# A spectral mixture and a rational expert layer: an add moved to GpSimd and two first-stage tasks moved ahead of the main loop

## Chip, cores and metric

The kernel runs on one core of a Trainium2 chip. The metric is the device time of one execution in microseconds; several executions were timed, and one was recorded by the profiler.

## What is computed

For each of 4 batches of 3008 rows and 256 columns, the reference takes a real Fourier transform over the rows, mixes the 256 columns with a complex matrix and a bias, shrinks real and imaginary part towards zero by 0.01, and transforms back. Each resulting row then goes through an expert layer with a rational activation:

```python
X = np.fft.rfft(x, axis=1)
Yr = Xr @ w_r - Xi @ w_i + b_r;  Yi = Xr @ w_i + Xi @ w_r + b_i
Yr, Yi = shrink(Yr, 0.01), shrink(Yi, 0.01)
y = np.fft.irfft(Yr + 1j * Yi, n=3008, axis=1).reshape(4 * 3008, 256)
h = y @ w_in                                   # 256 -> 2048
P = a[0] + a[1] * h + a[2] * h**2 + a[3] * h**3
Q = 1.0 + abs(b[0]) * abs(h) + abs(b[1]) * h**2
out = (P / (Q + 1e-06)) @ w_out                # 2048 -> 256
```

## The kernel before

**The transform.** 3008 = 64 x 47, and the transform of each batch is done in four stages of small matmuls. The stages of a batch pass data through DRAM twice: stage f1 writes s1, stage f2 reads it; stage i1 writes s2, the last stage (i2) reads it.

- f1 (`f1_task`, L185): 8 tasks per batch, one for each block c of 8 values of the 64. A task has 8 matmuls (L191) into two banks of PSUM, one copy by ScalarE (L155) and one by VectorE (L153) into a tile a, and stores of the tile to s1 by SyncE's DMA queue (L214 where the tile is whole, two stores; L217 where it is in parts, four stores).
- f2 (`f2_task`, L240): 12 tasks p. It reads a tile b of s1 (`load_b`, L227), does 8 matmuls (L247) and makes the tile x with ScalarE and VectorE.
- m (`m_task`, L268): 24 tasks, the mixing (L283) and shrinking.
- i1 (`i1_task`, L295): 12 tasks, stored to s2 (L308).

**The expert layer.** The result rows come in 26 groups of five blocks of 94 columns (two groups have four). For each group, `i2_task` (L338) does the last transform stage into a bank "pi" (L351), which ScalarE copies to xsh (L354) and VectorE makes into the remainder xsl (L362). For the last groups, when no transform task is left, the remainder comes from a matmul with a negative identity (L357) instead; the kernel calls such groups alone. Then 8 units per group follow, 208 in all. Unit u goes through:

- `g1_mm` (L369): 12 matmuls (L385) into h, a pair of banks; there are two such pairs. Unit 0 does its eight matmuls with xsh first, and the four with xsl after.
- `act_a` (L411), ScalarE: v = |b0 h| (L417), s = b1 h^2 (L418), then t (L421). Between them, an accumulating transfer on GpSimd's queue adds s to v (L419).
- `act_b` (L423), ScalarE: y = (v + C0)^2 (L426) and its inverse root (L428), so 1/Q.
- `dve_a` (L430), VectorE: two steps from t and h to t (L433, L434). After L434 the pair h is free for the unit after next.
- `dve_b` (L436): the high part of g (L442) and v (L444) on VectorE, t - v on GpSimd (L448), the low part of g on VectorE (L454).
- `g2_mm` (L460): 12 matmuls into the accumulators acc (L475), three iterations later.

**The order.** All engines' instructions are in an order written out by hand (`tc.manual_schedule()`). Ahead of the main loop, batch 0 goes through the whole transform, while the expert's weights are converted to high and low parts (`convert`, `from_f64`, L513 to L532; the tuples HC, HM and HF say how many steps of it come after which task). f1 tasks of batch 1 run there too: one at p = 13 (L694), and one for each entry of HF (L708 to L710). The order of blocks is 0, 1, 2, 3, 6, 7, 4, 5. Blocks 4 and 5 are loaded into the same slots as 0 and 1; these two loads wait in the list `hold` and go to SyncE's queue at the first `flush` of the loop.

The main loop (L735) has one iteration per unit, with a string that says the order of the steps: in iteration i TensorE gets the transform tasks that the planner picks (F), `g1_mm(i + 1)` and `g2_mm(i - 3)`. The planner gives each iteration a budget (`level` less the unit's own `load`) and takes tasks from the list while the spent cost stays under it; an f1 task uses both banks "ft", so there is at most one in an iteration. A task of cost 0 ends the iteration's picking. The list of batch 1 is: the f1 tasks that are left (each costs 0.95), the loads of the first two b tiles (cost 0), a pause (cost 0), f2 of p = 0 (0.86), a pause, and then f2, m and i1 tasks in turn.

**Memory.** Pools of the first part (pro, pro2, pro3; L506 to L509) are closed at L713. pro3 holds b_all (tags b0 to b3, the b tiles of batch 0), the tiles of x for batch 0, and blocks 2 and 3 of batch 1. pro holds the tiles a of the first four f1 tasks of batch 1 (the fourth in the tag "wt"). The pools mx (xsh, xsl) and mp (s, v, t, y, g) are opened on the freed space: mx lies on the beginning of pro3, mp on the rest of pro3 and on pro2 and pro. A pool's first writers wait for the closed pools that it lies on as whole pools. The pool sm stays open throughout: its tag "a" (3 slots of 128 x 512) holds parts of f1 tiles, i1 tiles and output tiles, its tag "x" (2 slots) the tiles x of later batches, f1 tiles of batches 2 and 3, and blocks 6 and 7 of batch 1.

Of the kernel before, what the change touches and what calls it, by code (L numbers as in the profile page):

```python
# [9 lines left out]
F32 = mybir.dt.float32  # L10
# [4 lines left out]
ALU = mybir.AluOpType  # L15
# [3 lines left out]
B, S, D, DFF = 4, 3008, 256, 2048  # L19
N1, N2, NG, NJ, NK = 64, 47, 2, 32, 24  # L20
ROWS = 2 * NK
JB = 5
TJ = NG * N2
# [5 lines left out]
WARM = 27  # L29
HC = (0, 0, 3, 3, 3, 3, 3, 3, 3, 3, 3, 3)  # L30
HM = (0, 0, 3, 4, 3, 4, 3, 4, 3, 4, 3, 4, 8, 0)
HF = (2, 3, 2)
I2Q = (5, 6)
SIZES = (5,) * 14 + (4,) + (5,) * 10 + (4,)
C0 = float(np.float32(1.0) + np.float32(1e-6))
# [64 lines left out]
def spectral_moe(ctx, tc, t, out):  # L100
    nc = tc.nc
# [5 lines left out]
    sm = pool("sm", 2)  # L107
# [15 lines left out]
    early = [1]  # L123
# [27 lines left out]
    def copy(eng, out, in_):  # L151
        if eng:
            nc.vector.tensor_copy(out, in_)  # L153
        else:
            nc.scalar.activation(out=out, in_=in_, func=ACTF.Copy)  # L155

    late = []
    hold = []
# [26 lines left out]
    def f1_task(b, c, pos):  # L185
        if pos == 0:
            new_s1(b)
        pts = [bank(b, "f1" if g else "") for g in range(NG)]
        for g, h in ((0, 0), (1, 1), (0, 1), (1, 0)):
            r = slice(64 * g, 64 * g + 48)  # L190
            nc.tensor.matmul(out=pts[g][64 * h:64 * h + 64], lhsT=f1[r],  # L191
                             rhs=xin[b, c][r, 2 * h:2 * h + 2, :].rearrange("p j d -> p (j d)"), start=True, stop=True)
        yield
        whole = None
        if early and pos < 4:
            whole = pro.tile([128, NG, 2, D], F32, tag="a" if pos < 3 else "wt", name="a", bufs=3 if pos < 3 else 1)
        elif b > 1:
            whole = sm.tile([128, 3, 2, D], F32, tag="x", name="a", bufs=2)[:, :NG]
        parts = [sm.tile([128, 2, D], F32, tag="a", name="a", bufs=3) if whole is None else whole[:, g] for g in range(NG)]
        for g in range(NG):  # L200
            copy(g if early or b == 1 else 0, parts[g].rearrange("p j d -> p (j d)"), pts[g])
        yield
        del xin[b, c]
        if b == 1 and c < 2:
            hold.append(lambda: load_x(b, c + 4))
        elif b > 1 and c + 2 < NJ // 4:
            load_x(b, c + 2)
        dst = s1[b].rearrange("k c g j d -> (k c) g j d")

        def send():  # L210
            for h in range(2):
                r, o = slice(64 * h, 64 * h + 48), slice(4 * c + 2 * h, 4 * c + 2 * h + 2)
                if whole is not None:
                    nc.sync.dma_start(out=dst[:, :, o], in_=whole[r])  # L214
                else:
                    for g in range(NG):
                        nc.sync.dma_start(out=dst[:, g, o], in_=parts[g][r])  # L217

        send() if direct or not early else sends.append(send)

    sends = []
# [94 lines left out]
    def load_first_c(k0, k1):  # L316
        if not first_c:
            first_c.append(sm.tile([96, JB, D], F32, tag="c", name="ct", bufs=1))
        r = slice(4 * k0, 4 * k1)
        nc.sync.dma_start(out=first_c[0][r], in_=s2[0].rearrange("k g c j d -> (k g c) j d")[r, :JB, :])  # L320
        c_t[0] = first_c[0]
# [14 lines left out]
    alone = {}  # L336

    def i2_task(n, ec):  # L338
        if ec == 0:
            alone[n] = nextb == B and not cur  # L340
            xs_t[n] = (mx.tile([128, 2, TB], F32R, tag="xsh", name="xsh"), mx.tile([128, 2, TB], F32R, tag="xsl", name="xsl"))
        xh, xl = xs_t[n]
        ct = c_t[n]
        w = len(blocks[n]) * TJ
        pt = ps.tile([128, 512], F32, tag="ft", name="pi2")
        last = len(blocks[n]) - 1
        for i in range(JB):
            z = slice(i * TJ, 512 if i == JB - 1 else (i + 1) * TJ)
            if i <= last or not alone[n]:
                k = min(i, last)  # L350
                nc.tensor.matmul(out=pt[:, z], lhsT=ct[:, k, ec * 128:(ec + 1) * 128], rhs=i2[:, :z.stop - z.start],  # L351
                                 start=i == 0, stop=True, skip_group_check=True)
        yield
        nc.scalar.activation(out=xh[:, ec, :w], in_=pt[:, :w], func=ACTF.Copy)  # L354
        yield
        if alone[n]:
            nc.tensor.matmul(out=pt[:, :w], lhsT=minus, rhs=xh[:, ec, :w], start=False, stop=True, skip_group_check=True)  # L357
            yield
            nc.scalar.activation(out=xl[:, ec, :w], in_=pt[:, :w], func=ACTF.Copy)
        else:  # L360
            yield
            nc.vector.tensor_tensor(out=xl[:, ec, :w], in0=pt[:, :w], in1=v32(xh[:, ec, :w]), op=ALU.subtract)  # L362
# [48 lines left out]
    def act_a(u):  # L411
        w = width(u)
        d = un[u]
        h = d["h"][:, :, :w]
        for nm, bufs in (("s", 2), ("v", 4), ("t", 4)):
            d[nm] = fresh(nm, bufs, u)
        nc.scalar.activation(out=d["v"], in_=h, func=ACTF.Abs, scale=rate["b0"])  # L417
        nc.scalar.activation(out=d["s"], in_=h, func=ACTF.Square, scale=rate["b1"])  # L418
        nc.gpsimd.dma_start(out=d["v"], in_=d["s"], accum_op=ALU.add)  # L419
        yield  # L420
        nc.scalar.activation(out=d["t"], in_=h, func=ACTF.Identity, scale=rate["a3"], bias=ca[:, 2:3])  # L421

# [63 lines left out]
    def drain(g):  # L486
        for _ in g:
            pass
# [18 lines left out]
    pro3 = pro_stack.enter_context(tc.tile_pool(name="pro3", bufs=3))  # L507
# [26 lines left out]
    with tc.manual_schedule():  # L534
# [61 lines left out]
        def convert(n):  # L596
            while n:
                if len(running) < 2 and len(done) < len(raws) and (not running or running[0][1] >= 2):
                    running.append([from_f64(*raws[len(done)]), 0])
                    done.append(1)  # L600
                if not running:
                    return
                pick = running.pop(0)
                pick[1] += 1
                n -= 1
                if pick[1] < STEPS:
                    next(pick[0])
                    running.append(pick)
                else:
                    drain(pick[0])  # L610
# [39 lines left out]
        for p in range(np_ + 3):  # L650
# [46 lines left out]
            if p == 8:  # L697
                for k, nm in enumerate(("b_r", "b_i")):
                    for z in range(2):
                        nc.sync.dma_start(out=offset[64 * k:64 * k + 64, z],  # L700
                                          in_=t[nm].rearrange("(o d) -> o d", o=1).to_broadcast([64, D]))
        load_rates()
        flush()
        load_first_c(NK - 2, NK)
        for send in sends:
            send()
        direct.append(1)
        for k in HF:  # L708
            drain(first.pop(0)[3])
            convert(k)  # L710
        assert not running and len(done) == len(jobs)
        late.extend(hold)
        pro_stack.close()  # L713
        mx = pool("mx", 2)
        mp = pool("mp", 2)
# [19 lines left out]
        for i in range(-1, nu + 4):  # L735
            flush()
            live = []
            parts = []
# [3 lines left out]
            if 0 <= i < nu:  # L742
                n, q = divmod(i, UB)
# [3 lines left out]
            for step in order.replace("m", "").replace("2", "2m").replace("1A", "Ao1") if nextb == B and not cur else order:  # L747
                if step == "F":
                    if 0 <= i < nu and n + 1 < nb and q in I2Q:
                        g = i2_task(n + 1, I2Q.index(q))  # L750
# [12 lines left out]
                    if cur:  # L763
                        budget += plan.pop(0) if plan else level
                        while cur and spent + cur[0][0] / 2 < budget and held + cur[0][1] <= 2 and not (live and storing(i)):
                            cost, use, free, g, part = cur.pop(0)
# [85 lines left out]
```

## Time and profile before

| | us |
|---|---|
| median of 3 runs (lowest, highest) | 1431.94 (1430.02, 1433.39) |
| the profiled execution | 1429.0 |
| its span | 1427.2 |
| TensorE busy | 1404.7 |
| VectorE busy | 1294.8 |
| ScalarE busy | 1135.6 |
| GpSimd busy | 668.9 |

The span runs from the first to the last recorded instruction. Busy time is the sum over an engine's instructions, overlaps counted once. In the rows below PE is TensorE, PEld its weight loads, ACT ScalarE, DVE VectorE, POOL GpSimd and SPq the DMA queue of SyncE. A timeline row has the start in us, the length in us (of the whole group where "xN" follows), engine, line, operation, and "out<-in" by the names in the program. Brackets hold the idle time of the engine before the row and what ended it; this releaser is inferred, and where an engine is named that had long been done, it was another. A matmul's end is modelled.

### The profile page before, as it was taken

To read this page: it belongs to the slowest core of one execution; us is meant where nothing else is said; L and a number is where in the kernel's file an instruction comes from. 1 tells how busy PE (TensorE), PEld (TensorE's weight loads), DVE (VectorE), ACT (ScalarE), POOL (GpSimd) and SP (SyncE) were. 2 spreads that over 40 slices of the span, in tenths; PEclk is the share of its full clock that TensorE was granted. 3 is DMA by queue.
4 is the path that set the end of the run, shared out by engine and by line. 5 is a ranking of instruction groups with operands and counts; after the bars stand their busy time and mean duration, and the time that the engine had idled before them with its cause. 6 is when DMAs were issued, how large, how long until landed. Compare 5 with 4: busy or idle time off the path is not lost.

```text
span 1427.2 us, 20352 instructions
## 1 busy us (share of the span) xinstructions
PE 1404.7 (98%) x7525; PEld 1232.4 (86%) x7525; DVE 1294.8 (91%) x1298; ACT 1135.6 (80%) x1439; POOL 668.9 (47%) x444
## 2 busy tenths in 40 slices
PE   9988999999999999999999999999999999999997
PEld 5966999999878999998888999999988888888887
DVE  3868889989899889999889999999999999999998
ACT  3768777788887787878888787888788998888985
POOL 0533444445454444454454444445455555555553
PEclk9999999999999999999999999999999999999999
DMA  9958445546686455546586455555455555555543
GB/s 333 383 189 170 103 104 129 114 89 148 141 205 160 108 108 117 110 102 142 134 213 153 96 122 108 115 116 108 92 124 112 106 115 103 110 113 105 113 80 79
DMA packets 84374, 191.58 MB, mean 134 GB/s; under 512 B 8556, under 2 KB 40468, under 8 KB 84276
## 3 DMA queue, kind: packets, MB, share of 16 engines
q0 software_dynamic: 29952, 98.58, 38.7%
q1 hardware_dynamic: 54212, 91.67, 19.3%
q8 instruction: 59, 0.97, 0.3%
q14 instruction: 39, 0.32, 0.1%
q10 hardware_dynamic: 112, 0.05, 0.0%
HBM read 54.21 MB, written 37.49 MB: 64 GB/s over the span
## 4 chain that ended last, share of the span: by engine, by line
PE 77%; DVE 11%; issue 8%; DMA 2%; ACT 2%; SPq 0%; DVEq 0%; ACTq 0%
PE h L385 29%; PE acc L475 29%; PE pft L283 7%; PE pi L351 4%; DVE t L433 3%; DVE v L444 3%; PE pft L247 2%; PE pft L301 2%; DVE g L442 1%; PE pft L191 1%; PE pft L174 1%; DVE t L434 1%; DVE g L454 1%; PE pm L283 1%; DVE e L525 1%
## 5 line engine op out<-in xcount | busy, mean ns | idle before, releaser
L475 PE MATMUL acc<-g,wsp 128*128 128x470 f32 (+1 forms) x2496 | 562.4, 374 | 3.4 <-DVE g L454 3.4
L448 POOL TENSOR_TENSOR t<-t,v 128x940 f32<-128x940 f32 (+1 forms) x206 | 478.5, 2323 | 137.8 <-DVE v L444 121.5
L475 PEld LDWEIGHTS acc<-g,wsp 128*128 128x128 f32 x2496 | 469.9, 190 | 62.5 <-DVE g L454 4.3
L385 PE MATMUL h<-xsh,win 128*128 128x470 f32 (+1 forms) x1664 | 433.3, 382 | 6.1 <-DVE t L434 5.6
L419 POOL DMA_DIRECT2D v<-s x208 | 183.6, 883 | 538.9 <-issue 501.3
L385 PEld LDWEIGHTS h<-xsh,win 128*128 128x128 f32 x1664 | 304.1, 190 | 61.6 <-PE acc L475 10.9
L417 ACT ACTIVATE v<-h 128x940 f32<-128x940 f32 (+1 forms) x208 | 196.1, 943 | 148.5 <-PE h L385 143.8
L442 DVE SCALAR_TENSOR_TENSOR g<-t,small,y 128x940 fp32r<-128x940 f32 (+1 forms) x208 | 255.2, 1227 | 51.1 <-ACT y L428 48.8
L433 DVE TENSOR_TENSOR t<-t,h 128x940 f32<-128x940 f32 (+1 forms) x208 | 231.4, 1112 | 24.7 <-ACT t L421 22.8
L434 DVE SCALAR_TENSOR_TENSOR t<-t,small,h 128x940 f32<-128x940 f32 (+1 forms) x208 | 245.2, 1179 | 7.4
L454 DVE SCALAR_TENSOR_TENSOR g<-t,small,y 128x940 fp32r<-128x940 f32 (+1 forms) x208 | 244.1, 1174 | 0.1
L385 PE MATMUL h<-xsl,win 128*128 128x470 f32 (+1 forms) x832 | 242.3, 373 | 0.0
L444 DVE SCALAR_TENSOR_TENSOR v<-v,g 128x940 f32<-128x940 f32 (+1 forms) x208 | 231.7, 1114 | 0.0
L421 ACT ACTIVATE t<-h,small 128x940 f32<-128x940 f32 (+1 forms) x208 | 215.6, 1036 | 0.0
L426 ACT ACTIVATE y<-v 128x940 f32<-128x940 f32 (+1 forms) x208 | 205.7, 989 | 8.1 <-DMA v<-s 8.0
L428 ACT ACTIVATE y<-y 128x940 f32<-128x940 f32 (+1 forms) x208 | 203.9, 980 | 2.4
L418 ACT ACTIVATE s<-h 128x940 f32<-128x940 f32 (+1 forms) x208 | 195.3, 939 | 0.0
L385 PEld LDWEIGHTS h<-xsl,win 128*128 128x128 f32 x832 | 156.1, 188 | 19.9
L283 PE MATMUL pft<-wrh,x 128*128 128x256 f32 x288 | 76.7, 288 | 0.2 <-ACT pft L155 0.2
L283 PE MATMUL pft<-wih,x 128*128 128x256 f32 x288 | 75.1, 283 | 0.0
L351 PEld LDWEIGHTS pi<-small,ct 96*128 96x128 f32 x516 | 65.7, 192 | 5.5 <-ACT a L155 3.0
L351 PE MATMUL pi<-small,ct 96*128 96x94 f32 (+1 forms) x516 | 66.9, 277 | 2.1 <-DMA ct<-s 2.1
(90 smaller groups left out, 1070.8 us busy)
## 6 DMA issues: line engine op xcount, KB each, us to landing
v<-s POOLq DMA_DIRECT2D x192, 470.0 KB, 4.5
xin<-in_x SPq DMA_DIRECT2D x30, 512.0 KB, 6.5
s<-zt SPq DMA_DIRECT2D x48, 256.0 KB, 3.5
out_t<-ob SPq DMA_DIRECT2D x48, 235.0 KB, 4.5
ct<-s SPq DMA_DIRECT2D x20, 480.0 KB, 5.5
bt<-s SPq DMA_DIRECT2D x36, 256.0 KB, 3.9
s<-a SPq DMA_DIRECT2D x42, 192.0 KB, 5.2
v<-s POOLq DMA_DIRECT2D x16, 376.0 KB, 4.0
```

Source lines behind the costliest of these rows:

```text
L283: nc.tensor.matmul(out=pt[:, k, :], lhsT=l, rhs=r, start=False, stop=n == len(ops) - 1, skip_group_check=True)
L385: nc.tensor.matmul(out=h[:, i, :w], lhsT=l, rhs=r, start=k == 0, stop=k == len(halves) // FU - 1)
L421: nc.scalar.activation(out=d["t"], in_=h, func=ACTF.Identity, scale=rate["a3"], bias=ca[:, 2:3])
L426: nc.scalar.activation(out=d["y"], in_=d["v"], func=ACTF.Square, bias=C0)
L428: nc.scalar.activation(out=d["y"], in_=d["y"], func=ACTF.Abs_reciprocal_sqrt)
L433: nc.vector.tensor_tensor(out=tt, in0=tt, in1=h, op=ALU.mult)
L434: nc.vector.scalar_tensor_tensor(out=tt, in0=tt, scalar=ca[:, 1:2], in1=h, op0=ALU.add, op1=ALU.mult)
L442: stt(out=hi, in0=tt, scalar=ca[:, 0:1], in1=y, op0=ALU.add, op1=ALU.mult)
L444: stt(out=v, in0=v, scalar=C0, in1=v32(hi), op0=ALU.add, op1=ALU.mult)
L448: nc.gpsimd.tensor_tensor(out=tt[:, :cut], in0=tt[:, :cut], in1=v[:, :cut], op=ALU.subtract)
L454: stt(out=lo, in0=tt, scalar=ca[:, 0:1], in1=y, op0=ALU.add, op1=ALU.mult)
L475: nc.tensor.matmul(out=acc[n][e][:, :w], lhsT=l, rhs=r, start=begun[n] == 1 and seen[e] == 1, stop=begun[n] == UB and seen[e] == 3 * FU)
```

## The change

Four things change. In the first three units, GpSimd adds s to v with an instruction of its own instead of issuing an accumulating transfer. HF gets two entries of 0, so two more f1 tasks of batch 1 (blocks 6 and 7) run ahead of the loop, with tiles in the tags b2 and b3 of pro3; two (blocks 4 and 5) are left for the loop, and their tiles are whole ones in the tag "x" of sm, stored with two transfers instead of four. The loads of blocks 4 and 5 are issued ahead of the stores of block 0 and block 2 instead of at the loop's start. And in groups that are alone, the fifth matmul of pi has 94 columns instead of 136.

```diff
@@
-HF = (2, 3, 2)
+HF = (2, 3, 2, 0, 0)
@@ def f1_task
         whole = None
         if early and pos < 4:
             whole = pro.tile([128, NG, 2, D], F32, tag="a" if pos < 3 else "wt", name="a", bufs=3 if pos < 3 else 1)
-        elif b > 1:
+        elif early and pos < 6:
+            whole = pro3.tile([128, 3, 2, D], F32, tag=f"b{pos - 2}", name="a", bufs=1)[:, :NG]
+        else:
             whole = sm.tile([128, 3, 2, D], F32, tag="x", name="a", bufs=2)[:, :NG]
-        parts = [sm.tile([128, 2, D], F32, tag="a", name="a", bufs=3) if whole is None else whole[:, g] for g in range(NG)]
         for g in range(NG):
-            copy(g if early or b == 1 else 0, parts[g].rearrange("p j d -> p (j d)"), pts[g])
+            copy(g if early or b == 1 else 0, whole[:, g].rearrange("p j d -> p (j d)"), pts[g])
@@
                 r, o = slice(64 * h, 64 * h + 48), slice(4 * c + 2 * h, 4 * c + 2 * h + 2)
-                if whole is not None:
-                    nc.sync.dma_start(out=dst[:, :, o], in_=whole[r])
-                else:
-                    for g in range(NG):
-                        nc.sync.dma_start(out=dst[:, g, o], in_=parts[g][r])
+                nc.sync.dma_start(out=dst[:, :, o], in_=whole[r])
@@ def i2_task
-            z = slice(i * TJ, 512 if i == JB - 1 else (i + 1) * TJ)
+            z = slice(i * TJ, 512 if i == JB - 1 and not alone[n] else (i + 1) * TJ)
@@ def act_a
-        nc.gpsimd.dma_start(out=d["v"], in_=d["s"], accum_op=ALU.add)
+        if u < 3:
+            nc.gpsimd.tensor_tensor(out=d["v"], in0=d["v"], in1=d["s"], op=ALU.add)
+        else:
+            nc.gpsimd.dma_start(out=d["v"], in_=d["s"], accum_op=ALU.add)
@@ ahead of the loop
         load_first_c(NK - 2, NK)
+        hold.pop(0)()
         for send in sends:
             send()
         direct.append(1)
         for k in HF:
             drain(first.pop(0)[3])
+            while hold:
+                hold.pop(0)()
             convert(k)
         assert not running and len(done) == len(jobs)
-        late.extend(hold)
         pro_stack.close()
```

## Rows read from the trace of the kernel before

**Rows 1.** The page, busy time, share of the span and instructions of each engine

```profile
...
PE 1404.7 (98%) x7525; PEld 1232.4 (86%) x7525; DVE 1294.8 (91%) x1298; ACT 1135.6 (80%) x1439; POOL 668.9 (47%) x444
...
```

**Rows 2.** Windows: PE, PEld, DVE, ACT, POOL busy, then granted PE clock

```profile
...
98.80:103.00 4.20, 4.20 (x18) 3.01 (x17) 0.77 (x2) 0.56 (x1) 0.16 (x1) 0.66 0.94 276
...
115.80:132.40 16.60, 15.77 (x69) 12.58 (x70) 16.46 (x16) 14.82 (x18) 9.03 (x6) 0.91 0.84 175
132.40:200.00 67.60, 67.31 (x393) 61.16 (x392) 59.62 (x64) 50.23 (x65) 28.18 (x19) 1.00 0.54 120
...
```

**Rows 3.** Timeline of TensorE, 91 to 134 us: start, length, instruction

```profile
...
91.15 3.01 PE L191 MATMUL pft<-xin,small 48*64 48x512 f32 x24
96.28 2.87 PE L351 MATMUL pi<-small,ct 96*128 96x94 f32 x20 [2.12 <-DMA ct<-s]
98.79 3.39 PE L385 MATMUL h<-xsh,win 128*128 128x470 f32 x8
...
115.77 1.94 PE L385 MATMUL h<-xsh,win 128*128 128x470 f32 x4 [1.19 <-DVE t L434]
...
127.15 1.08 PE L385 MATMUL h<-xsh,win 128*128 128x470 f32 x4 [0.83 <-DVE t L434]
...
133.70 1.13 PE L247 MATMUL pft<-f,bt 128*128 128x128 f32 x8
...
```

**Rows 4.** Timeline of ScalarE, 94 to 126 us

```profile
...
94.44 1.07 ACT L155 ACTIVATE a<-pft 128x512 f32<-128x512 f32 x2
96.99 0.63 ACT L530 ACTIVATE wsp<-e 128x512 fp32r<-128x512 f32 x1 [1.47 <-DVE e L525]
97.68 0.56 ACT L354 ACTIVATE xsh<-pi 128x470 fp32r<-128x470 f32 x1
...
103.28 0.95 ACT L417 ACTIVATE v<-h 128x940 f32<-128x940 f32 x1 [3.53 <-DMA s<-a]
...
106.86 0.95 ACT L417 ACTIVATE v<-h 128x940 f32<-128x940 f32 x1 [0.36 <-PE h L385]
...
111.75 0.99 ACT L426 ACTIVATE y<-v 128x940 f32<-128x940 f32 x1 [1.67 <-DMA v<-s]
...
119.97 0.95 ACT L417 ACTIVATE v<-h 128x940 f32<-128x940 f32 x1 [1.22 <-PE h L385]
...
125.00 0.94 ACT L417 ACTIVATE v<-h 128x940 f32<-128x940 f32 x1
...
```

**Rows 5.** Timeline of SyncE's DMA issues, 94 to 129 us

```profile
...
94.51 5.43 SPq L214 DMA_DIRECT2D s<-a  x8
100.03 1.46 SPq L148 DMA_DIRECT2D xin<-in_x  x2
...
128.51 23.36 SPq L227 DMA_DIRECT2D bt<-s  x5
...
```

**Rows 6.** DMA issues, 94 to 104 us and 84 to 200 us: median landing last

```profile
...
s<-a SPq DMA_DIRECT2D x8, 192.0 KB, 3.5
...
bt<-s SPq DMA_DIRECT2D x8, 256.0 KB, 5.3
...
```

**Rows 7.** Timeline of VectorE, 106 to 119 us

```profile
...
106.10 1.13 DVE L433 TENSOR_TENSOR t<-t,h 128x940 f32<-128x940 f32 x1 [1.26 <-DMA xin<-in_x]
...
112.76 0.69 DVE L153 COPY a<-pft 128x512 f32<-128x512 f32 x1 [4.29 <-ACT y L426]
...
118.51 1.12 DVE L433 TENSOR_TENSOR t<-t,h 128x940 f32<-128x940 f32 x1
...
```

**Rows 8.** Timeline of GpSimd, 118 us

```profile
...
118.08 2.21 POOL L448 TENSOR_TENSOR t<-t,v 128x940 f32<-128x940 f32 x1 [1.50 <-DVE v L444]
...
```

**Rows 9.** Groups of TensorE by form: L351; and line L357

```profile
...
L351 PE MATMUL pi<-small,ct 96*128 96x94 f32 x416 | 53.7, 272 | 2.1 <-DMA ct<-s 2.1
...
L351 PE MATMUL pi<-small,ct 96*128 96x136 f32 x100 | 21.6, 298 | 0.0
...
L357 PE MATMUL pi<-xsh,minus x14: 333/374/381, 1097.6 to 1370.9; 128*128 128x470 f32 x12, 128*128 128x376 f32 x2
...
```

## The prediction

> **What bounds the kernel now.** I read the page first: TensorE is busy 98% of the span [rows 1], so whatever work TensorE can't put beside something else is time. Then the stretches. From 132.4 us on it is busy 67.31 of 67.60 us [rows 2]; there is nothing to win there except by giving it less to do. It loses time at the loop's start, and the timeline of that stretch shows where [rows 3]: 2.12 us before the first pi (waiting for the last part of ct), unit 0's eight high matmuls in 3.39 us (0.42 us each, at a granted clock of 0.66 of full speed over that stretch [rows 2]), and short waits for VectorE to free an h bank (1.19 at 115.77, 0.83 at 127.15).
>
> The other engines tell why [rows 4, 7]. ScalarE writes v of unit 0 at 103.28 after a wait that ended with the stores s<-a; y of unit 0 starts at 111.75, 1.67 us late, when the accumulating transfer has landed (issued near 105.7, so 6 us); VectorE stands still for 4.29 us until 112.76. Those 6 us are what the change goes for. But v at 103.28 is also a row against it: v lies on no byte of the tiles a that these stores read. It waited because mp lies on the freed pools, and in the program as built the first writer in a new pool waits for all users of the pools beneath it, here for the eight stores. mx (xsh, xsl) lies on pro3 alone, and pro3's last transfers were loads long done, so the xsh copy at 97.68 waited for none.
>
> **The change, part by part.**
>
> *Two tasks moved ahead, their tiles in pro3.* Per task TensorE has 8 matmuls (24 in 3.01 us for three [rows 3], so 1.0 us), ScalarE and VectorE a copy each, SyncE two stores. TensorE's 2 us fit in the 2.12 us that it waits for ct, but the two ScalarE copies stand behind the conversion at 96.99 (0.63) and then take 1.07 [rows 4]: the second ends near 98.7, pi needs those banks, and xsh would start near 99.6 instead of 97.68: 1.9 us late.
>
> The tiles are b2 and b3 of pro3. So now the stores of these two tasks read pro3, and the first writer of mx, the xsh copy, has to wait until they have landed. On SyncE's queue stand, from 94.51: the loads of blocks 4 and 5 (moved ahead of the stores) and twelve stores instead of eight. A store takes 5.43 / 8 = 0.68 us of the queue, a load 1.46 / 2 = 0.73 [rows 5]: 12 x 0.68 + 2 x 0.73 = 9.6 us. The last issue begins at 103.4 and lands 3.5 us later [rows 6]: **xsh at 107.0, 9.3 us late**. Lower bound: an empty queue, the last copy at 98.7 + 0.7 + 3.5 = 102.9. Upper: 12 x 0.197 + 2 x 0.524 MB = 3.4 MB at the 276 GB/s of that stretch [rows 2], 12.4 us, plus a landing's tail: 109. I take 107.0, since the issue pace is the row of the same instruction.
>
> *Unit 0.* Before, its twelve matmuls took 4.2 us, partly at the lower clock [rows 2]. After, TensorE idles from about 101 (end of pi) to 107.6, then does the same: 0.6 (the copy) + 4.2 us, and v of unit 0 comes at 111.8 instead of 103.28: 8.5 late. Bounds for the twelve: 2.5 (half of 0.42 each) to 5.0 (0.42 each [rows 3]). The Trainium skill (TensorE: Matmul & The Clock Gate, "HAM oscillation — how this bites in real kernels") says that matmuls which start after a long wait for a DMA start cold, at half clock; by that rule all twelve would take 5.0 and v would come at 112.6. The rows have such a fall after a shorter wait, so the trace agrees in kind; the sum goes by 4.2.
>
> *GpSimd adds for units 0 to 2.* An add costs GpSimd 2.21 us (the same shape as L448 [rows 8]) where the transfer took 6 to land. GpSimd is half idle [rows 1]. In unit 2 its queue has the add ahead of L448 of unit 0, which starts some 2 us later; VectorE meanwhile has L442 of unit 1, so I count nothing (up to 0.6 if that cover is too short). VectorE's 4.29 us go too, and nothing of ScalarE waits for a DMA: v of unit 1 is 3.6 us after v of unit 0 (one task and one unit of TensorE, as 106.86 - 103.28), v of unit 2 one ScalarE round later, 5.0 (125.00 - 119.97) [rows 4], and L433 follows its v by 2.8 (106.10 - 103.28) [rows 4, 7]. So L433 of unit 2 starts at 111.8 + 3.6 + 5.0 + 2.8 = 123.2; before, 118.51 [rows 7]. **3.8 of the 8.5 come back; 4.7 stay.** What is late next is VectorE's release of the h banks, as before.
>
> *Two tasks fewer in the loop.* With two left, blocks 4 and 5 run in iterations 0 and 1, the loads of b follow, and the first f2 task comes in iteration 3 instead of 5. In TensorE's queue it stands ahead of unit 4. Block 5's copies end near 118.7 (v of unit 1 at 115.4, its s and t, the copy), its last store is issued at 119.4 and lands at 122.9, and the b load takes 0.4 to issue and 5.3 to land [rows 6]: near 128.6 (before, these loads were issued from 128.51 [rows 5] and f2 ran at 133.70 [rows 3]). Unit 4 could start when L433 and L434 of unit 2 are done, 123.2 + 2.3 = 125.5. A new wait of up to 3.1 us; 0.8 of it takes the place of the wait at 127.15, and f2's 0.9 us is work done early: net 1.4 (0 to 3, as the b load takes 3.5, like a store, or the clock falls again).
>
> *Stores.* One per half instead of two in the loop; SyncE is not the limit there. Using tag x for a: its two slots held blocks 6 and 7, read by then. Nothing.
>
> *Narrower last pi matmul.* Of the 14 tasks of L357, 12 lose 42 columns; 298 - 272 = 26 ns each [rows 9], 0.3 us. Bounds 0 and 0.6.
>
> **Sum:** 4.7 + 1.4 - 0.3 = +5.8 us. Against the profiled execution, 1429.0 (its span of 1427.2 and 1.8 around it, which the change doesn't touch), that is 1434.8; the median of the runs stands 2.9 us above that execution, so 1431.94 + 5.8 = **1437.7**.
>
> **The rivals.**
> *The xsh copy doesn't wait for the stores* (only what lies under its own bytes counts). Against it: v of unit 0 waited in this way. Then xsh is 1.9 late, but v still waits for the twelve stores, 107.0 instead of 103.28: 3.7 - 3.8 + 1.4 - 0.3 = +1.0, 1432.9. Chance 0.14.
>
> *Neither waits, and the start simply gets shorter: not slower.* xsh at 99.6, v of unit 0 at 104.4, 1.1 late; 3.8 come back in the first three units, f2 finds its b tile and fills TensorE's idle time (-0.9), -0.3: -3.9, 1428.0. It decides at v of unit 0: while that comes before about 107, the 6 us transfers taken away outweigh what is added ahead; later, the added wait does. For it speaks that the transfer is plainly waited for at 111.75; against it the same pool rule, at two places. Chance 0.08.
>
> *The wait is longer and the clock falls twice*: landing at 109, twelve cold matmuls and the full f2 wait: 6.7 + 0.8 + 3.0 - 0.3 = +10.2, 1442.1. It belongs to the forecast's own range. That the change doesn't move the tasks at all I exclude: the two zeros drain the next two tasks of the list whatever the planner does.
>
> **How the numbers follow.** Forecast (stores waited for at xsh) 0.75, nearly all of it slower; its low end (landing at 102.9) is 5.8 - 4.1 = +1.7. About 0.2%, 2.9 us, is what a measurement of this kernel can tell from no change. Slower 0.74 (the forecast with a landing after 104, and some left over for what I haven't seen), same 0.18 (the first rival and the forecast's low end), faster 0.08 (the second). Range 1431.5 to 1442.5: from the first rival less the spread of the runs up to the bounds of landing, clock and f2; the second rival is left outside.
>
> **What would show it.** Right: ScalarE's first L354 waits several us for DMA s<-a and starts after 104; TensorE has one idle stretch of about 7 us before unit 0 with that end; y of unit 0 waits for nothing; L433 of unit 2 follows v of unit 0 by about 11.4 us instead of 15.2; f2 (L247) of iteration 3 waits for bt. Wrong: L354 starts near 99.6, or v of unit 0 before 107, or TensorE's start-up loss spread elsewhere and the same shift missing after 140 us.

## The result and the profile after

The changed kernel takes 1441.14 us (median of 4 runs, 1440.2 to 1443.91), the kernel before beside it 1432.47 (4 runs, 1430.02 to 1433.39). The ratio is 1.0066, with a 95% interval of 1.0047 to 1.0085, or 6.7 to 12.2 us slower; by the medians it is 8.7. The forecast was +5.8 us, 1437.7, with a range of 1431.5 to 1442.5. The time lies inside the range, 3.4 us above the forecast; 0.5 of that is the start of the sum (1431.94 was the median of three runs of the kernel before, with the fourth it is 1432.47).

The profiled execution of the kernel after took 1440.2 us, with a span of 1438.4: 11.2 us more than that of before. Busy times on the page, against [rows 1]:

```profile
PE 1403.3 (98%) x7524; PEld 1233.8 (86%) x7525; DVE 1297.3 (90%) x1298; ACT 1135.7 (79%) x1439; POOL 673.3 (47%) x444
```

TensorE is busy 1.4 us less than before, so on balance the loss is idle time. The waits of TensorE say which. The columns are: engine, tile and line that waited, what it waited for, us in all, how many times, the longest. Before:

```profile
PE h L385 <- DVE t L434: 5.6, 17, 1.2
PE acc L475 <- DVE g L454: 3.4, 3, 2.2
...
PE pi L351 <- DMA ct<-s: 2.1, 1, 2.1
...
PE pft L283 <- ACT pft L155: 0.2, 1, 0.2
```

After (behind L214 a line has a number lower by 3, L348 for L351 for instance; from the transfer L419 on they are the same again):

```profile
PE h L382 <- ACT xsh L351: 7.9, 1, 7.9
PE acc L475 <- DVE g L454: 4.7, 4, 2.2
PE h L382 <- DVE t L434: 4.6, 17, 0.9
PE pft L280 <- ACT pft L155: 2.8, 1, 2.8
...
PE pft L244 <- DMA bt<-s: 2.7, 2, 1.6
```

All rows of this view together make 17.9 us before and 30.8 after: 12.9 more, and less 1.4 of busy time that is 11.5, nearly the 11.2. Three waits are new or have grown: one of 7.9 us for the xsh copy, one of 2.8 for a bank "pft" (0.2 before), and 2.7 for b tiles in the loop. The wait for ct has gone.

**The start.** ScalarE's timeline, against [rows 4]:

```profile
108.25 1.02 ACT L351 ACTIVATE xsh<-pi 128x470 fp32r<-128x470 f32 x2 [9.37 <-DMA s<-a]
113.08 0.95 ACT L414 ACTIVATE v<-h 128x940 f32<-128x940 f32 x1 [3.82 <-issue]
...
119.91 1.02 ACT L426 ACTIVATE y<-v 128x940 f32<-128x940 f32 x1
...
135.82 0.60 ACT L155 ACTIVATE pft<-offset 128x512 f32<-128x512 f32 x1 [4.35 <-DVE x L252]
```

The first xsh copy stands still for 9.37 us until the stores s<-a have landed. SyncE's queue shows what it waits for, against [rows 5]:

```profile
94.78 0.35 SPq L148 DMA_DIRECT2D xin<-in_x  x1
95.19 2.79 SPq L214 DMA_DIRECT2D s<-a  x4
98.07 0.55 SPq L148 DMA_DIRECT2D xin<-in_x  x1
98.73 22.53 SPq L214 DMA_DIRECT2D s<-a  x12
```

Of the last group eight belong to the tasks ahead of the loop. The chain of waits (start, us, what) goes through the landing of the last of these, which is issued from 104.45, right behind the one at 103.85, and has landed at 108.07:

```profile
103.85 0.55 SPq L214
...
104.45 3.62 DMA s<-a
```

TensorE's timeline, against [rows 3]:

```profile
88.80 1.09 PE L191 MATMUL pft<-xin,small 48*64 48x512 f32 x8
...
98.45 2.52 PE L348 MATMUL pi<-small,ct 96*128 96x94 f32 x20 [1.14 <-ACT a L155]
108.86 3.28 PE L382 MATMUL h<-xsh,win 128*128 128x470 f32 x8 [7.90 <-ACT xsh L351]
111.98 1.01 PE L382 MATMUL h<-xsl,win 128*128 128x470 f32 x4
...
126.49 1.13 PE L244 MATMUL pft<-f,bt 128*128 128x128 f32 x8 [1.58 <-DMA bt<-s]
...
136.47 0.58 PE L280 MATMUL pft<-wrh,x 128*128 128x256 f32 x1 [2.84 <-ACT pft L155]
```

**After the start.** y of unit 0, at 119.91, waits for nothing: the transfer's 1.67 us and VectorE's 4.29 [rows 4, 7] are gone, as the change wanted. The bracket in [rows 7] and the prediction put the 4.29 down to y and its transfer, but the copy L153 that ended them writes a tile a and uses neither v nor y. It was the fourth part of two f1 tasks, for which the tag "a" of sm has three slots; a store of the first part was issued at 107.38 and took 5.3 us to land, and the copy came at 112.76. After the change these tiles are whole ones in another tag, and the copy at 118.19 waits for nothing. In e3 below, where the parts are still there, the profile names the store.

But two things come later that were not there before. VectorE:

```profile
123.28 1.14 DVE L444 SCALAR_TENSOR_TENSOR v<-v,g 128x940 f32<-128x940 f32 x1
124.60 1.13 DVE L433 TENSOR_TENSOR t<-t,h 128x940 f32<-128x940 f32 x1 [0.18 <-ACT t L421]
...
126.88 2.77 DVE L442 SCALAR_TENSOR_TENSOR g<-t,small,y 128x940 fp32r<-128x940 f32 x1
...
135.10 0.68 DVE L252 TENSOR_TENSOR x<-pft,x 128x512 fp32r<-128x512 f32 x1
```

GpSimd:

```profile
123.70 2.78 POOL L417 TENSOR_TENSOR v<-v,s 128x940 f32<-128x940 f32 x1 [2.78 <-ACT s L415]
126.44 2.21 POOL L448 TENSOR_TENSOR t<-t,v 128x940 f32<-128x940 f32 x1
```

First, the step L442 of unit 1 takes 2.77 us instead of 1.19 while GpSimd's L448 of unit 0 runs; L448 stands there because the add of unit 2 is ahead of it on GpSimd (e6 tests this). Second, the first mixing task runs some iterations earlier. It needs a bank that ScalarE fills with an offset (135.82); that copy stands behind VectorE's L252 at 135.10, which stands behind VectorE's late steps. TensorE waits 2.84 us and then runs this task at half clock (granted 0.50, which is 1.2 GHz). Windows of the kernel after (from:to, length, busy of PE, PEld, DVE, ACT, POOL with counts, then granted clock, DMA share, GB/s):

```profile
100.98:108.86 7.88, 0.00 (x0) 0.00 (x0) 0.01 (x1) 0.61 (x2) 0.00 (x0) 0.75 0.70 250
108.86:113.00 4.14, 4.13 (x16) 3.34 (x20) 1.19 (x2) 0.41 (x1) 0.00 (x0) 0.65 0.01 4
...
136.50:142.20 5.70, 5.70 (x25) 5.61 (x26) 4.10 (x5) 3.45 (x4) 3.11 (x2) 0.50 0.41 77
```

The 24 mixing matmuls take 5.66 us at 0.50, where the first task of before took 3.14 at full clock.

**A ledger by unit.** One instruction per unit makes a clock for the whole kernel: L434 on VectorE, 208 times. Units 2, 7 and 40, before:

```profile
119.67 1.19 DVE L434 SCALAR_TENSOR_TENSOR t<-t,small,h 128x940 f32<-128x940 f32 x1
...
151.25 1.19 DVE L434 SCALAR_TENSOR_TENSOR t<-t,small,h 128x940 f32<-128x940 f32 x1
...
382.73 1.19 DVE L434 SCALAR_TENSOR_TENSOR t<-t,small,h 128x940 f32<-128x940 f32 x1
```

The same units after:

```profile
125.77 1.19 DVE L434 SCALAR_TENSOR_TENSOR t<-t,small,h 128x940 f32<-128x940 f32 x1
...
166.28 1.19 DVE L434 SCALAR_TENSOR_TENSOR t<-t,small,h 128x940 f32<-128x940 f32 x1
...
392.03 1.19 DVE L434 SCALAR_TENSOR_TENSOR t<-t,small,h 128x940 f32<-128x940 f32 x1
```

The delay is 6.1 us at unit 2, 15.0 at unit 7, 9.3 at unit 40 and 11.2 at unit 207, the last. At unit 7 part of it is work done early (f2 and mixing tasks that before came later), which is paid back by unit 20 (10.2). Of every one of these 0.3 is the part ahead of the loop: the first f1 task of batch 1 starts at 88.51 before and 88.80 after. The last 1.9 come behind unit 40: 2.3 up to unit 100, of which 0.4 is paid back later. They are not the change's: units 40 to 100 took 2.6 us longer than in that one execution in a run of the kernel before with another kind of wait (e8 below), and 2.1 in one with the adds alone (e3). So the pair of profiles shows about 9 us for the change, as the medians do.

### The profile page after: what moved, and what is told of

It is laid out like the page before. It is cut to its first block, busy times and chain, and to the rows that moved or that the text cites. A ratio compares the mean times of both kernels' runs of the same rounds, so it can differ in the third digit from the quotient of the medians.

```text
span 1438.4 us, 20331 instructions
## 1 busy us (share of the span) xinstructions
PE 1403.3 (98%) x7524; PEld 1233.8 (86%) x7525; DVE 1297.3 (90%) x1298; ACT 1135.7 (79%) x1439; POOL 673.3 (47%) x444
## 4 chain that ended last, share of the span: by engine, by line
PE 75%; DVE 11%; issue 8%; DMA 3%; ACT 3%; SPq 1%; DVEq 0%; ACTq 0%
PE h L382 29%; PE acc L475 28%; PE pft L280 7%; PE pi L348 4%; DVE t L433 3%; DVE v L444 3%; PE pft L298 2%; PE pft L244 2%; PE pft L191 1%; DVE g L442 1%; PE pft L174 1%; DVE t L434 1%; DMA s<-a 1%; DMA s<-zt 1%; DVE e L525 1%
## 5 line engine op out<-in xcount | busy, mean ns | idle before, releaser
L448 POOL TENSOR_TENSOR t<-t,v 128x940 f32<-128x940 f32 (+1 forms) x206 | 477.6, 2318 | 132.9 <-DVE v L444 117.2
L419 POOL DMA_DIRECT2D v<-s x205 | 181.0, 883 | 530.3 <-issue 483.3
L442 DVE SCALAR_TENSOR_TENSOR g<-t,small,y 128x940 fp32r<-128x940 f32 (+1 forms) x208 | 257.3, 1237 | 53.9 <-ACT y L428 51.7
L433 DVE TENSOR_TENSOR t<-t,h 128x940 f32<-128x940 f32 (+1 forms) x208 | 231.6, 1114 | 26.1 <-ACT t L421 25.2
L434 DVE SCALAR_TENSOR_TENSOR t<-t,small,h 128x940 f32<-128x940 f32 (+1 forms) x208 | 245.2, 1179 | 7.4
L444 DVE SCALAR_TENSOR_TENSOR v<-v,g 128x940 f32<-128x940 f32 (+1 forms) x208 | 232.0, 1115 | 0.1
L348 PEld LDWEIGHTS pi<-small,ct 96*128 96x128 f32 x516 | 65.6, 192 | 4.3 <-ACT a L155 2.0
L348 PE MATMUL pi<-small,ct 96*128 96x94 f32 (+1 forms) x516 | 66.0, 275 | 1.1 <-ACT a L155 1.1
```

What stands on the lines that cost most here:

```text
L433: nc.vector.tensor_tensor(out=tt, in0=tt, in1=h, op=ALU.mult)
L434: nc.vector.scalar_tensor_tensor(out=tt, in0=tt, scalar=ca[:, 1:2], in1=h, op0=ALU.add, op1=ALU.mult)
L442: stt(out=hi, in0=tt, scalar=ca[:, 0:1], in1=y, op0=ALU.add, op1=ALU.mult)
L444: stt(out=v, in0=v, scalar=C0, in1=v32(hi), op0=ALU.add, op1=ALU.mult)
L448: nc.gpsimd.tensor_tensor(out=tt[:, :cut], in0=tt[:, :cut], in1=v[:, :cut], op=ALU.subtract)
```

## The experiments

Each kernel was timed in turn with the kernel before. "us" is the difference of its median to that of the kernel before beside it (1431.95 us for e1 to e4, 1431.66 for e5 to e8, 1432.41 for e9 to e11). The ratio is that of the means, so the two can differ by a microsecond. e2, e4, e6 and e7 ran 5 times, the other experiments 11 or 12 times.

| run | edit | us | ratio [95%] |
|---|---|---|---|
| after | | +8.7 | 1.0066 [1.0047, 1.0085] |
| e1 | after, waits by tile | +3.1 | 1.0019 [1.0008, 1.0029] |
| e2 | after, two more pauses | +8.2 | 1.0055 [1.0041, 1.0069] |
| e3 | before, with the three adds alone | +0.9 | 1.0003 [0.9994, 1.0012] |
| e4 | after, without the adds | +10.9 | 1.0077 [1.0062, 1.0093] |
| e5 | e1, the two tiles in other tags | +1.1 | 1.0001 [0.9989, 1.0013] |
| e6 | after, two adds instead of three | +10.5 | 1.0068 [1.0053, 1.0083] |
| e7 | after, two loads behind the stores | +9.7 | 1.0063 [1.0049, 1.0078] |
| e8 | before, waits by tile | +1.8 | 1.0008 [0.9999, 1.0017] |
| e9 | e5, two more pauses | -2.0 | 0.9984 [0.9974, 0.9993] |
| e10 | e5, one more pause | -3.0 | 0.9977 [0.9968, 0.9985] |
| e11 | e9, without the adds | -2.1 | 0.9984 [0.9975, 0.9994] |

### e1: does the xsh copy wait because of the pool?

```diff
-        mx = pool("mx", 2)
-        mp = pool("mp", 2)
+        mx = pool("mx", 2, reuse_waits="tile")
+        mp = pool("mp", 2, reuse_waits="tile")
```

With this a tile waits only for the freed tiles that lie under its own bytes.

> The changed kernel, with the pools mx and mp waiting only for the old tiles that lie under a new tile's own bytes, and no longer for whole closed pools. Theory (the loss begins at the xsh copy that waits for twelve stores): the first L351 starts near 99.6 us with no DMA ahead of it; s of unit 0 still waits for block 6's stores, since it lies on b2, so v and s of unit 0 come at 105 to 108; the early f2 and m tasks keep their own cost. Time about 1434.5, 6 to 7 us under the changed kernel. Rival (the work moved ahead and the new order of the tasks cost the time, whatever the wait): the wait goes, and the time stays at 1439 or more.

ScalarE's timeline of e1:

```profile
101.36 0.56 ACT L351 ACTIVATE xsh<-pi 128x470 fp32r<-128x470 f32 x1 [0.99 <-PE pi L348]
...
110.12 0.95 ACT L414 ACTIVATE v<-h 128x940 f32<-128x940 f32 x1 [7.07 <-DMA s<-a]
```

The copy no longer waits for stores, and 5.6 us by the medians (6.7 by the ratios) are gone, as the expectation had it. It comes 11.08 us after the first f1 task of batch 1 (90.28 here), where it came at 9.17 before: these 1.9 us are the two tasks' own. v of unit 0 still waits 7.07 us, of which about 4.6 lie behind the end of its matmuls (105.5): the tiles b2 and b3 do lie under s and v. So the wait of the copy was the pool's and not the data's, and it is the larger part of the loss.

### e8: the same edit without the change

The edit of e1 on the kernel before, as a control.

> The kernel before with tile-wise waits of mx and mp alone, as a control for the runs that have them. Theory: v of unit 0 waited for the eight stores by at most 0.3 us longer than for its own matmuls, so nothing changes: 1432, within 1 us of the kernel before. Rival (tile-wise waits change the order or save waits elsewhere): 2 us or more under it.

No gain: +1.8 us by the medians, and the interval holds 1. What e1 wins, it wins from the wait that the change made.

### e7: fewer issues ahead of the last store

```diff
@@ ahead of the loop
-        hold.pop(0)()
...
-            while hold:
-                hold.pop(0)()
...
+        late.extend(hold)
```

The loads of blocks 4 and 5 go behind all twelve stores.

> The changed kernel with the loads of blocks 4 and 5 issued at the loop's start again, behind all twelve stores. Theory (the stores' landing ends the wait, and the DMA engines were full, 320 to 360 GB/s from 102 to 106 us): 1.05 MB less ahead of the last store, so the first L351 starts 2 to 3 us earlier, near 105.5, and the time falls by 2 to 3 us to 1438.5. Rival (SyncE's issue pace sets the landing): two issues of 0.5 us less, the first L351 about 1 us earlier, the time within 1.5 us of the changed kernel. In both, TensorE has the blocks in time.

```profile
107.21 1.02 ACT L351 ACTIVATE xsh<-pi 128x470 fp32r<-128x470 f32 x2 [7.72 <-DMA s<-a]
```

Counted from the first f1 task of batch 1 (89.40 here), ScalarE's copy comes at 17.81 instead of 19.45, so 1.6 earlier, between what the theory (2 to 3) and the rival (about 1) said: 0.9 is the issuing of the two loads, 0.35 and 0.55 us above, and the stores were issued faster too. The twelve matmuls of unit 0 then took longer (v follows their start by 4.91 us instead of 4.22, at a lower clock). The median, 1441.35, is that of the change, so the theory's 2 to 3 us did not come; a gain of one us or so can't be told by these intervals.

### e3: the adds alone

```diff
@@ act_a, on the kernel before
-        nc.gpsimd.dma_start(out=d["v"], in_=d["s"], accum_op=ALU.add)
+        if u < 3:
+            nc.gpsimd.tensor_tensor(out=d["v"], in0=d["v"], in1=d["s"], op=ALU.add)
+        else:
+            nc.gpsimd.dma_start(out=d["v"], in_=d["s"], accum_op=ALU.add)
```

> The kernel before with GpSimd's add in the first three units and nothing else of the change. Theory: y of unit 0 no longer waits for a transfer and VectorE loses less than the 4.3 us at 112; 2 to 4 us under the kernel before, about 1429.5. Rival (VectorE's copy at 112.76 waited for the stores of the parts of block 6, which still are there, and nothing comes back): 1432, the same as before. A second rival: GpSimd's adds hold up VectorE's steps with two inputs from SBUF, 1 to 2 us slower than before.

The time shows nothing of it (1.0003): the theory's 2 to 4 us did not come. By the trace the adds do what they were to do: L433 of unit 2 comes 27.30 us after the first f1 task of batch 1, where it came at 30.00 before, 2.7 earlier. Most of this is then given back; in the ledger 1.7 is left at unit 3 and 1.0 from unit 8 to unit 40. Lines of e3 are higher by 3, so its L445 and L451 are L442 and L448 of before. VectorE:

```profile
111.52 0.69 DVE L153 COPY a<-pft 128x512 f32<-128x512 f32 x1 [1.11 <-DMA s<-a]
...
120.05 2.11 DVE L445 SCALAR_TENSOR_TENSOR g<-t,small,y 128x940 fp32r<-128x940 f32 x1
```

GpSimd:

```profile
118.95 2.21 POOL L451 TENSOR_TENSOR t<-t,v 128x940 f32<-128x940 f32 x1
```

TensorE:

```profile
127.33 1.16 PE L385 MATMUL h<-xsh,win 128*128 128x470 f32 x4 [1.84 <-DVE t L437]
```

The first row is the copy that stood still for 4.29 us before: here it waits 1.11, and for a store, as the first rival said of its cause. The second is the same long step of VectorE as after the change, 2.11 us beside GpSimd; then come a wait of 1.84 us for an h bank and a few matmuls at the lower clock. The second accumulation starts 41.05 us after that first f1 task, against 41.28 before. So the waits in units 2 to 5 are for VectorE, not for the transfer.

### e4: the change without the adds

```diff
-        if u < 3:
+        if u < 0:
```

> The changed kernel with accumulating transfers in all units, the first three too. Theory (3.8 us of the shift at unit 0 come back through the adds): 2 to 4 us above the changed kernel, 1443 to 1445. Rival (the adds are worth nothing, or cost as much by holding up VectorE as they save): within 1 us of the changed kernel, 1441.

1442.87 us, 1.7 more than the change by the medians, though the intervals overlap. y waits again for the transfer (0.30 and 1.42 us), and the first f2 task waits 5.44 us for its b tile:

```profile
133.47 2.04 PE L244 MATMUL pft<-f,bt 128*128 128x128 f32 x8 [5.44 <-DMA bt<-s]
```

So the adds are worth 1.6 to 2.2 us where the start is late, if anything (the intervals don't part them from nothing), and they are not the cause of the loss. L433 of unit 2 follows v of unit 0 by 12.08 us here (116.05 to 128.13), against 11.52 with the adds and 15.23 before: most of what came back at the start came without the adds.

### e6: is the third add what holds VectorE up?

```diff
-        if u < 3:
+        if u < 2:
```

> The changed kernel with GpSimd's add in units 0 and 1 only, unit 2 by transfer. Theory (L442 of unit 1 took 2.77 us instead of 1.19 because GpSimd's L448 of unit 0, pushed back by the add of unit 2, ran at the same time): that L442 takes 1.2 us, the third L434 comes 1.5 us earlier, y of unit 2 doesn't wait long for its transfer; 0 to 1.5 us under the changed kernel. Rival (VectorE and GpSimd don't hold each other up; L442 was long for another reason): L442 still near 2.8 us.

VectorE:

```profile
128.33 1.34 DVE L442 SCALAR_TENSOR_TENSOR g<-t,small,y 128x940 fp32r<-128x940 f32 x1
```

ScalarE:

```profile
133.61 0.99 ACT L426 ACTIVATE y<-v 128x940 f32<-128x940 f32 x1 [2.60 <-DMA v<-s]
```

Without the third add GpSimd's L448 of unit 0 is 2.16 us under way when L442 starts, instead of 0.44, and L442 falls from 2.77 to 1.34 us: the cause of that length is shown. But y of unit 2 now waits 2.60 us for its transfer, and the time is no better (1442.13, where up to 1.5 us less was expected). A loss of 1.6 us went, and a wait of 2.6 came.

### e2: the first f2 and mixing tasks later again

```diff
-        ts += [(0.0, 0, 0, load_first(b), 0)] + [(0.0, 0, 0, iter(()), 0)]
+        ts += [(0.0, 0, 0, load_first(b), 0)] + [(0.0, 0, 0, iter(()), 0)] * (3 if b == 1 else 1)
```

Two more pauses in the list of batch 1 put these tasks back to where they were before.

> The changed kernel with two more pauses in the list of batch 1, so that the first f2 task runs in iteration 5 as before the change. Theory: the xsh wait stays (first L351 near 108), but TensorE no longer waits for bt, nor 2.8 us ahead of the first m task, and that task runs at 0.12 us per matmul instead of 0.21: 2 to 4 us under the changed kernel, about 1438. Rival (the whole shift comes from the xsh wait, and what TensorE loses at the first m task it would lose elsewhere): 1441, no change beyond 1 us.

The mixing task's wait is gone, it runs at full clock, and in the ledger the delay is flat, 8.45 us from unit 3 to unit 15 (1.6 of that lies ahead of the loop in this execution). But waits for L434 rise from 4.6 to 8.3 us. The median is 1440.11, 1.0 us less than that of the change (1.6 by the ratios, and the intervals overlap). The theory's 2 to 4 us did not come: in this kernel, whose start is late anyway, the early tasks cost about one us, if the times can tell it at all.

### e5: neither the copy nor v waits

```diff
@@ f1_task, on e1
-            whole = pro3.tile([128, 3, 2, D], F32, tag=f"b{pos - 2}", name="a", bufs=1)[:, :NG]
+            whole = pro3.tile([128, NG, 2, D], F32, tag=f"x{pos - 2}", name="a", bufs=1)
```

The tiles of blocks 6 and 7 go to slots of pro3 under other tiles than s and v.

> The changed kernel with tile-wise waits of mx and mp, and the tiles of blocks 6 and 7 in pro3's slots of blocks 2 and 3, which lie under t of units 1 and 2 and not under xsh, v or s. Theory (only the two waits for the twelve stores make the start late): first L351 without a DMA ahead of it, v of unit 0 within 1 us of the end of its matmuls, some 4 us earlier than with the tile-wise waits alone; by the sum of the prediction's second rival 1428 to 1430, under the kernel before. Rival (VectorE sets the pace of the first units, 5.5 us for each, and what comes earlier is given back by the time TensorE is full): 1431 to 1433, the same as before.

1432.75, the time of before (1.0001). v of unit 0 waits for TensorE alone:

```profile
106.53 0.95 ACT L414 ACTIVATE v<-h 128x940 f32<-128x940 f32 x1 [2.49 <-PE h L382]
```

So the waits on stores, at the copy and at v, account for the whole of the loss, within the 1.7 us of the interval. The expectation, 1428 to 1430, was missed, and the rival's 1431 to 1433 came. They do not account for a gain that should now be there: the first accumulation comes 2.9 us earlier than before, counted from the first f1 task. The timeline of TensorE shows where that goes:

```profile
119.88 1.13 PE L244 MATMUL pft<-f,bt 128*128 128x128 f32 x8 [1.48 <-DMA bt<-s]
...
129.95 0.39 PE L280 MATMUL pft<-wrh,x 128*128 128x256 f32 x1 [2.92 <-ACT pft L155]
```

### e9, e10, e11: the early tasks and the adds, with the start mended

e9 is e5 with the two pauses of e2, e10 has one of them:

```diff
@@ e10, on e5
-        ts += [(0.0, 0, 0, load_first(b), 0)] + [(0.0, 0, 0, iter(()), 0)]
+        ts += [(0.0, 0, 0, load_first(b), 0)] + [(0.0, 0, 0, iter(()), 0)] * (2 if b == 1 else 1)
```

> The kernel of the tile-wise waits with blocks 6 and 7 in pro3's slots of blocks 2 and 3, and two more pauses in the list of batch 1, so that the first f2 task runs in iteration 5. Theory (that kernel's first accumulation stood 2.9 us earlier than before, counted from the first f1 task of batch 1, and gave it back when the first m task waited 2.9 us and ran at the lower clock): no wait ahead of the first m task, its matmuls at 0.12 us each, and 1.5 to 2.5 us under the kernel before, 1429.5. Rival (VectorE sets the pace of the first units, so that TensorE loses the same time in waits for L434): within 1 us of the kernel before.

> The same with one more pause, so that the first f2 task runs in iteration 4. Theory: between the kernel without a pause and that with two; if the m task still finds its bank held by VectorE's L252 the 2.9 us wait stays and the time is that of the kernel before (1432), if not, 1 to 2 us under it. Rival: as with two pauses, no change.

e9 takes 1430.46 us and e10 1429.44, both below the kernel before, with intervals that leave 1 out. e10 is the fastest of all kernels here, 3.0 us under before. Against e5 the pauses win 2.4 to 3.4 us by the ratios, of which e9's 2.4 is barely clear of noise (the intervals of e5 and e9 overlap a little): with an early start the early f2 and mixing tasks cost about that much. TensorE's waits in e10:

```profile
PE h L382 <- DVE t L434: 7.4, 18, 2.2
```

The wait for the offset's bank isn't among its rows; waits for VectorE remain, 1.8 us more for h than before.

e11 is e9 with the transfers back in all units.

> The kernel with two pauses and accumulating transfers in all units. Theory (the adds bring y of unit 0 forward, worth 1.7 us in the changed kernel): 1 to 2.5 us above the kernel with two pauses and adds. Rival (with VectorE as the pace, and GpSimd's L448 beside L442 holding VectorE up by 1.6 us, the adds are worth nothing): within 0.8 us of it.

1430.36 us, as e9. y waits 0.55 and 0.94 us for transfers, and L442 takes 1.20 us instead of 2.75. So there the adds and what they do to VectorE cancel: an edit meant to take away 6 us of latency is worth nothing.

## Why the prediction was right, and where its sizes were off

**Right: the copy waits for the stores of the two moved tasks.** The forecast had it at 107.0; it came at 108.25. The last of twelve stores and two loads was issued from 104.45 (forecast 103.4) and had landed 3.62 us later (forecast 3.5). The queue began 0.3 us later than in the sum, and thirteen issues took 9.67 us instead of 8.9: that makes the difference. e1 shows that this wait was the pool's. The row with which the forecast argued for it says less than it was read to say: v of unit 0 at 103.28 [rows 4] came right behind its own matmuls as well, which ended at 103.03:

```profile
102.02 1.01 PE L385 MATMUL h<-xsl,win 128*128 128x470 f32 x4
```

That the kernel before loses nothing by the pool's wait is what e8 shows. So the rule was right, and that row was no proof of it. The first rival (v waits and the copy doesn't) was built in e1: it gave +3.1 us where the rival said +1.0. The second (neither waits) was built in e5 and gave the time of before where the rival said -3.9; it is nearly reached only when the early tasks are put back too (e10, -3.0).

**Right: unit 0 at a lower clock.** v follows the first of its twelve matmuls by 4.22 us (forecast 4.2 and the bounds 2.5 to 5.0). In four other kernels with a like idle stretch (6.3 to 8.0 us) it was 4.26 (e2), 4.91 (e7), 5.16 (e4) and 5.16 (e6). In all five the granted clock was 0.50 to 0.54 over the first eight, which is the lower level, 1.2 GHz; over the last four it was 1.00 in after and e2, 0.62 in e7 and 0.50 in e4 and e6. That the sum's 4.2 was met so closely is therefore partly luck: it was taken from a row behind a wait of 2.12 us, and in e4 and e6 the same matmuls took 5.16. The Trainium skill (TensorE: Matmul & The Clock Gate, "HAM oscillation — how this bites in real kernels") says that matmuls behind a long wait for a DMA start cold, at half clock; these five traces agree with that start, and all twelve at half clock, the 5.0 of the prediction, came in e4 and e6 alone.

**Right in size, not in cause: what comes back in the first three units.** v of unit 0 was 9.8 us late (113.08 against 103.28 [rows 4]), L433 of unit 2 at 124.60 was 6.1 late ([rows 7]: 118.51). That is 3.7 given back; the forecast said 3.8. L433 follows v of unit 0 by 11.52 us (forecast 11.4). But the prediction put this down to the adds. Without them L433 follows v by 12.08 us in e4 and 12.22 in e11, instead of the 15.23 of before; with the adds alone it follows by 12.44 (e3). Each takes away most of the same stop, VectorE's 4.29 us for a store, and the whole tiles in tag x, which the prediction priced as "Nothing", gave 3.1 of the 3.7 without the adds. That the sum came out is luck here. With the later landing 5.8 us stay instead of 4.7 (6.1 less the 0.3 ahead of the loop): the first mis-sized term.

**Mis-sized: GpSimd's adds as free.** The forecast's cover was VectorE's L442 of unit 1, "up to 0.6 if that cover is too short". That step was not a cover: beside L448 it took 2.77 us instead of 1.19, so it lost 1.58. It holds up the L434 behind it: the delay in the ledger goes from 6.1 at unit 2 to 7.1 at unit 3. The trace of the kernel before had such a step already, L442 at 978.08 (below).

**Mis-sized: "net 1.4" for the earlier f2.** f2 does wait for its b tile, until 126.49 instead of 128.6: the b loads were issued at 123.65 and took under 3 us instead of 5.3, and 1.58 us are lost instead of 3.1. What the step left out is the task behind f2. The first mixing task came earlier too, waited 2.84 us for its bank and lost 5.66 - 3.14 = 2.5 us to the clock. By the ratios the early tasks together cost 1.6 (after against e2) to 3.4 us (e5 against e10); by the ledger at unit 40, 2.2 (after against e2) and 1.4 (e5 against e9).

**The narrower matmul: nothing instead of 0.3.** Between the first and the last L357 [rows 9] 273.3 us pass before and 273.2 (1108.9 to 1382.1) after, though 24 matmuls are narrower (100 of 136 columns before, 76 after), not 12. In that stretch VectorE is as busy as TensorE, which may be why; no run has this part of the change alone. The window 1090:1410 of after:

```profile
1090.00:1410.00 320.00, 316.96 (x1548) 278.64 (x1547) 316.93 (x291) 282.15 (x335) 178.02 (x117) 1.00 0.54 108
```

So the change cost 2.9 us more than the forecast's 5.8. In the ledger 1.1 of that is the later start (5.8 instead of 4.7), 0.3 the matmuls, and 1.8 lie between units 2 and 40 (3.2 instead of 1.4), with VectorE's long step and the mixing task. How those divide is open: the runs price both only together with what takes their place (e2, e6).

## To carry to other kernels

Before a late producer gets a buffer from a pool that is about to be freed, look up who first writes to the memory after it: a wait by pool turns a store of 192 KB into a stop of the whole core, and a longer list of transfers ahead of it makes that stop longer. Work that fills one idle stretch early also brings forward the work behind it in the list; follow it until the orders agree again, through every engine that it needs. When a profile names what ended an idle stretch, look up what the instruction reads and writes: VectorE's copy needed a slot, not the y that was named. And when a latency goes, ask which engine is then the next to be late: here VectorE, which left 1.0 of the 2.7 us that the adds won, too little for the times to show.

## What the runs showed of the hardware

**VectorE stands still beside GpSimd.** L442 (t and y in SBUF) that starts while GpSimd's L448 runs ends 1.00 us after L448's end, though their overlap differs (1.77 us in after, 1.11 in e3, 1.19 in e1, 1.75 in e5): in after L448 ends at 126.44 + 2.21 = 128.65 and L442 at 126.88 + 2.77 = 129.65; in e3 121.16 and 122.16; in e1 126.64 and 127.64; in e5 122.10 and 123.10. So nearly the whole overlap is lost, not a share of it. The kernel before has it as well, with an overlap of 0.83 us (L448 from 976.38, 2.53 long):

```profile
978.08 1.84 DVE L442 SCALAR_TENSOR_TENSOR g<-t,small,y 128x940 fp32r<-128x940 f32 x1
```

It goes the other way too: the third add began at 123.70, beside VectorE's L444 (until 124.42), and took 2.78 us instead of 2.22. The steps L433 and L434, with h in PSUM, ran beside GpSimd at 1.12 and 1.19 us, which they take alone too (131.73 and 132.88 beside L448 at 131.90).

The Trainium skill (SBUF — State Buffer, "Who interferes with whom") has this as an exclusive lock: an instruction of VectorE with two inputs in SBUF and one of GpSimd that reads SBUF block each other, and the one that issues first goes on. These rows agree: L442 and L444 have two inputs in SBUF, and whichever began later lost the time.

**The same order, two clocks.** e5 and e10 reach unit 0 through the same tasks, with gaps of 0.92 and 1.14 us (e5) and 0.93 and 1.13 us (e10) on TensorE. In windows of 100 to 103 and 103 to 107 us the granted clock was 1.00 and 1.00 in e5, 0.76 and 0.76 in e10. v of unit 0 comes 15.27 us after the first f1 task of batch 1 in e5 and 16.48 in e10. So part of what separates two single executions of nearly the same kernel, 1.2 us here, is not in the kernel, and single profiles can't settle a difference of that size.
